# Background weight conversions in four pieces a unit, handed out inside the gated products

## The chip, the core and the metric

The kernel runs on one NeuronCore of a Trainium2 chip. The time is device microseconds of one execution. The engines that matter here are TensorE (matmuls, PE in the rows; PEld is its weight load), VectorE (DVE), ScalarE (ACT), GpSimd (POOL) and SyncE (SP), whose queue issues nearly all DMAs. Each engine takes its queue in the order in which the program emits it.

## The reference

Softcapped attention, then two MLPs on its output, in fp32 (inputs come as 64-bit floats):

```python
scores = cap * np.tanh(scale * q @ k.T / cap)              # 4 x 12 heads, 448 x 64
x = softmax(scores) @ v                                    # -> 1792 tokens x 768
g = sigmoid(x @ w_gate) * (x @ w_val)                      # "first MLP", d_ff 1536
y = g @ w_out                                              # 1792 x 768
h = y @ w_in2                                              # "second MLP", d_ff 2048
out = (h * np.cos(h)) @ w_out2                             # 1792 x 768
```

## The kernel before

The tokens go in two halves of 896 (two batches each). The order of all instructions is written out by hand: the program's order is each engine's order. First comes attention for the first half, then the gated MLP for it, `mlp1(0, ...)`, with the second half's attention beside it; then `mlp1(1, ...)`, the second gated MLP, which is the stretch that the change touches; then the cosine MLP for the second half and for the first, `mlp2(1, ...)` and `mlp2(0, ...)`.

Every product is done in three matmul passes of split fp32 operands: high weight by high input, high weight by low input, low weight by high input (`mm3`, six matmuls of 448 columns per 128 rows of contraction). So a weight tile needs a split before TensorE can use it: `w_split` lets ScalarE write the high part (L233) and GpSimd the low part (L234). A tile of gate or value weights, or half of an output column block's, feeds one product of 36 matmuls.

The weights arrive as 64-bit floats. Converting one unit of them (128 x 768 values, some units half as large) takes a raw load of 768 KB (`raw_tile`, L147), two ScalarE instructions (`signs`: Abs, L156, then Sign, L158) and four VectorE instructions (`convert`, L163 to L173). In `mlp1(0, ...)` the gated MLP's units are converted as they are used, and stored (`kept`). `mlp1(1, ...)` only loads them again (`f<-kept`, L140) and splits them. Meanwhile it converts the 34 units of the cosine MLP in the background and stores them in `kept` (L203), for both passes of `mlp2`: the first 6 units of input weights, 6 of output weights, 5, 6, 5 and 6; units 19, 22, 30 and 33 among them, counted from 0, are half-size.

`background()` is a generator; each `next(beside, None)` hands out one piece of it. A unit is three pieces: (1) Abs, Sign, the store of the unit before and the raw load of the unit after; (2) two VectorE instructions; (3) the other two. The very first piece loads the first raw tile.

`mlp1` loops over the 12 hidden units m (128 columns of d_ff each): the gate's product, its sigmoid on ScalarE, `w_step()`; the value product, gate times value on VectorE, the split of the result (`copy` on ScalarE, subtraction on VectorE), `w_step()`. `w_step` emits the split of the weights that TensorE needs two products later (`lead[0] = 2`), then, with `w_loads`, the load of the kept tile that is split two steps after. After each hidden unit come five pieces. Then come the six output blocks m, two products each, with a piece after some of the twelve contraction steps, a `w_step` after each product and the split of y at the end (copy on ScalarE, subtraction on VectorE). What is left of the background is emitted after the last block.

Kept tiles `f` and background results `fb` share four buffers (`fpool`), which go round in the order in which they were released; raw tiles and split weights share seven (`wts`).

Of the kernel before, what the change touches and what calls it, by code (L numbers as in the profile page):

```python
# [27 lines left out]
def softcap_attention_gated_mlp_cos_mlp(  # L28
# [40 lines left out]
    BESIDE = ((2, 10), (3, 2), (3, 6), (4, 1), (4, 5), (4, 8), (5, 1), (5, 5), (5, 8))  # L69


    PIECES, BESIDE_Y = 5, (0, 2, 4, 6, 8, 9, 11)

    AGAIN = (1, 2, 4, 5, 7, 8, 10, 11)

# [19 lines left out]
    def big_tile(shape, dtype, name):  # L95
        return big.tile(shape, dtype, tag="big", name=name)
# [33 lines left out]
    def f_tile(i):  # L130
        return fpool.tile([P, UW], F32, tag="f", name=f"f{i}")
# [12 lines left out]
    def raw_tile(u):  # L144
        name, src, nk, n = u
        t = wts.tile([P, UW, 2], I32, tag="w", name=f"{name}_raw")[:, : nk * n]
        nc.sync.dma_start(out=t.rearrange("p (k f) t -> p k f t", k=nk), in_=src)  # L147
        return t
# [5 lines left out]
    def signs(raw, g):  # L154
        hi = raw[..., 1].bitcast(F32)
        nc.scalar.activation(out=g, in_=hi, func=AF.Abs)  # L156
        yield
        nc.scalar.activation(out=hi, in_=hi, func=AF.Sign, bias=tiny)  # L158

    def convert(raw, g):  # L160
        lo, hi = raw[..., 0], raw[..., 1]
        gi = g.bitcast(I32)
        nc.vector.tensor_scalar(out=g, in0=g, scalar1=F64_MIN_HI, scalar2=F64_MAX_HI, op0=ALU.max, op1=ALU.min)  # L163
        yield
        nc.vector.tensor_scalar(
            out=gi, in0=gi, scalar1=4, scalar2=REBIAS, op0=ALU.logical_shift_left, op1=ALU.bitwise_xor
        )
        yield
        nc.vector.scalar_tensor_tensor(
            out=gi, in0=lo, scalar=28, in1=gi, op0=ALU.logical_shift_right, op1=ALU.bitwise_or  # L170
        )
        yield
        nc.vector.scalar_tensor_tensor(  # L173
            out=gi, in0=gi, scalar=1, in1=hi, op0=ALU.logical_shift_right, op1=ALU.bitwise_xor
        )
# [20 lines left out]
    def background():  # L196

        raw = {N1: raw_tile(unit[N1])}
        done = None

        def store():
            u, g = done
            nc.sync.dma_start(out=kept[u][:, : g.shape[1]], in_=g)  # L203
            there.add(u)

        yield
        for u in range(N1, NU):
            _, _, nk, n = unit[u]
            g = f_tile(f"b{u}")[:, : nk * n]
            for _ in signs(raw[u], g):  # L210
                pass
            if done:
                store()
            if u + 1 < NU:
                raw[u + 1] = raw_tile(unit[u + 1])
            yield
            c = convert(raw.pop(u), g)
            next(c)
            next(c)
            yield  # L220
            for _ in c:
                pass
            done = (u, g)
            yield
        store()
# [52 lines left out]
    def w_step(mid=nothing):  # L278

        w_front(mid)  # L280
        w_back()
# [22 lines left out]
    def w_catch():  # L304

        if pos["split"] < min(pos["use"] + min(3, lead[0]), pos["conv"]):
            w_back()
        if pos["conv"] < min(pos["use"] + 5, pos["split"] + 3):
            w_front()

    def w_take():
        i = pos["use"]
        pos["use"] += 1
        return w_t.pop(i)
# [190 lines left out]
    def mm3(ps, w, kk, x, first, last):  # L505

        for wi, xi in ((0, 0), (0, 1), (1, 0)):
            for c in range(BH):
                nc.tensor.matmul(  # L509
                    ps[:, c, :S],  # L510
                    lhsT=w[:, wi, kk, :],
                    rhs=x[:, xi, c, :],
                    start=(first and (wi, xi) == (0, 0)),
                    stop=(last and (wi, xi) == (1, 0)),
                )

    def ps_tile(name):
        return psS.tile([P, BH, 512], F32, tag="S", name=name)

    def tmp_tile(name):  # L520
        return tmp.tile([P, BH, S], F32, tag="tmp", name=name)

    def mlp1(hf, before, beside):

        x = [x_t[i] for i in range(KD)]
        g = []
        for m in range(KF):
            ps = {}  # L530
            for part in ("g", "v"):
                w = w_take()
                ps[part] = ps_tile(f"p{part}{hf}_{m}")
                if m == 0:
                    for kk in range(KD - 2):
                        mm3(ps[part], w, kk, x[kk], kk == 0, False)
                    if part == "g":
                        w_first = w
                        for _ in before:
                            pass  # L540
                        continue
                    for kk in (KD - 2, KD - 1):
                        mm3(ps["g"], w_first, kk, x[kk], False, kk == KD - 1)
                    sg = tmp_tile(f"sg{hf}_{m}")
                    nc.scalar.activation(out=sg, in_=ps["g"][:, :, :S], func=AF.Sigmoid)
                    w_step()
                    for kk in (KD - 2, KD - 1):
                        mm3(ps["v"], w, kk, x[kk], False, kk == KD - 1)
                else:
                    for kk in range(KD):  # L550
                        mm3(ps[part], w, kk, x[kk], kk == 0, kk == KD - 1)
                    if part == "g":
                        sg = tmp_tile(f"sg{hf}_{m}")
                        nc.scalar.activation(out=sg, in_=ps["g"][:, :, :S], func=AF.Sigmoid)
                        w_step()
            nc.vector.tensor_tensor(out=sg, in0=ps["v"][:, :, :S], in1=sg, op=ALU.mult)  # L556
            gt = big_tile([P, 2, BH, S], F32R, f"g{hf}_{m}")
            nc.scalar.copy(out=gt[:, 0], in_=sg)  # L558
            nc.vector.tensor_tensor(out=gt[:, 1], in0=sg, in1=gt[:, 0].bitcast(F32), op=ALU.subtract)
            g.append(gt)  # L560
            w_step()
            w_catch()
            if hf:
                for _ in range(PIECES):
                    next(beside, None)
        y = []
        for m in range(KD):
            ps = ps_tile(f"py{hf}_{m}")
            for s in range(2):
                w = w_take()  # L570
                for kk in range(KF // 2):
                    i = s * KF // 2 + kk
                    mm3(ps, w, kk, g[i], i == 0, i == KF - 1)
                    if hf == 0 and (m, i) in BESIDE or hf and i in BESIDE_Y:
                        next(beside, None)
                w_step()
            if hf == 0:
                yt = tmp_tile(f"y{hf}_{m}")
                nc.scalar.copy(out=yt, in_=ps[:, :, :S])
                nc.sync.dma_start(out=ykept[m], in_=yt)  # L580
                continue
            yt = big_tile([P, 2, BH, S], F32R, f"y{hf}_{m}")
            nc.scalar.copy(out=yt[:, 0], in_=ps[:, :, :S])
            nc.vector.tensor_tensor(out=yt[:, 1], in0=ps[:, :, :S], in1=yt[:, 0].bitcast(F32), op=ALU.subtract)
            y.append(yt)
        return y
# [132 lines left out]
    with tc.manual_schedule():  # L719
        nc.vector.memset(zeros, 0.0)  # L720
        nc.vector.reciprocal(out=tanh_scale, in_=cap_sb)
        nc.vector.tensor_scalar_mul(out=tanh_scale, in0=tanh_scale, scalar1=1.0 / float(D) ** 0.5)
        nc.scalar.activation(out=guard, in_=cap_sb, func=AF.Exp, scale=-1.0)
        nc.vector.tensor_scalar_mul(out=guard, in0=guard, scalar1=1e-9 / CP)
        att = [attention(hf) for hf in range(B // BH)]
        steps = 3 + (BH * NP + 1) * NC - LAST
        for _ in range(steps):
            next(att[0])
        mlp1(0, att[0], att[1])
        for _ in range(steps - len(BESIDE)):  # L730
            next(att[1])
        others = background()
        lead[0] = 2
        y = mlp1(1, att[1], others)
        y_first = []
        for _ in others:
            pass
        lead[0] = 3
        mlp2(1, y, y_again(y_first))
        mlp2(0, y_first, iter(()))  # L740
# [35 lines left out]
```

## Time and profile before

| | |
|---|---|
| time, median of 3 runs | 1235.0 us (1234.67, 1235.0, 1239.3) |
| the profiled execution: time, span | 1240.16 us, 1238.4 us |
| TensorE busy, of the span | 1208.6 us, 98% |
| VectorE, ScalarE, GpSimd busy | 55%, 48%, 36% |
| mean granted TensorE clock, of full speed | 0.993 |

Busy shares are of one profiled execution. A matmul's end is modelled, so a busy TensorE is not one at its peak; the starts of its groups of matmuls tell its pace.

### The profile page before, as it was taken

The page shows a single profiled execution, that of the slowest core. Times are in us where ns is not written, and L with a number is a line of the kernel's source. Part 1 is how long each engine was busy: PE and PEld are TensorE (multiplying, and loading weights), DVE is VectorE, ACT ScalarE, POOL GpSimd, SP SyncE. Part 2 cuts the span into 40 slices and gives each one's busy share as a digit, 9 for nine tenths or more (in the row PEclk, how much of TensorE's full clock was granted, in tenths as well). Part 3 has the DMA queues.
Part 4 walks back from the last instruction along what each step waited for, and adds up shares of the span by engine and source line. Part 5 has one row for each costly group of instructions (what it writes and reads, how often), then busy time and mean ns, then how long its engine had stood idle before and what let it go on. Part 6 is the DMA issues. An engine that isn't in the chain of part 4 may idle for free. (4 is left out here: it accounts for less than half of the span.)

```text
span 1238.4 us, 15883 instructions
## 1 busy us (share of the span) xinstructions
PE 1208.6 (98%) x6342; PEld 1037.4 (84%) x6342; DVE 682.1 (55%) x729; ACT 593.7 (48%) x664; POOL 443.4 (36%) x234
## 2 busy tenths in 40 slices
PE   8989999999999999999899899999999999999998
PEld 4445889999987546989888799999999999999998
DVE  6998698777633996555555674420423434024242
ACT  6886555445426885444343544533505335244150
POOL 2767132232314675222212221622424334235040
PEclk9999999999999999999999899999999999999999
DMA  6432465545833340455554675221121531212013
GB/s 154 126 94 69 156 209 171 167 159 164 216 129 107 90 124 1 153 167 177 179 179 155 208 248 167 64 64 43 48 77 33 167 120 52 77 32 88 22 33 96
DMA packets 127082, 148.17 MB, mean 120 GB/s; under 512 B 50080, under 2 KB 100640, under 8 KB 127008
## 3 DMA queue, kind: packets, MB, share of 16 engines
q1 hardware_dynamic: 126720, 147.09, 38.8%
q8 instruction: 50, 0.82, 0.3%
q14 instruction: 24, 0.20, 0.1%
q10 hardware_dynamic: 288, 0.07, 0.0%
HBM read 112.13 MB, written 35.00 MB: 119 GB/s over the span
## 5 line engine op out<-in xcount | busy, mean ns | idle before, releaser
L234 POOL TENSOR_TENSOR w<-f,w 128x768 fp32r<-128x768 f32 (+1 forms) x140 | 267.5, 1916 | 683.3 <-ACT w L233 598.5
L631 PE MATMUL po<-w,z 128*128 128x384 f32 x1248 | 220.8, 334 | 2.2 <-POOL w L234 2.2
L631 PEld LDWEIGHTS po<-w,z 128*128 128x128 f32 x1248 | 216.8, 188 | 3.0 <-POOL w L234 2.8
L509 PE MATMUL pg<-x,w 128*128 128x448 f32 x864 | 185.1, 372 | 7.2 <-ACT w L233 4.6
L509 PEld LDWEIGHTS pg<-x,w 128*128 128x128 f32 x864 | 164.0, 191 | 25.5 <-ACT w L233 5.7
L509 PE MATMUL py<-g,w 128*128 128x448 f32 x864 | 181.7, 371 | 3.3 <-ACT w L233 2.3
L509 PE MATMUL pv<-x,w 128*128 128x448 f32 x864 | 181.2, 367 | 1.0 <-DVE sg L556 1.0
L509 PEld LDWEIGHTS py<-g,w 128*128 128x128 f32 x864 | 163.8, 191 | 18.9 <-ACT w L233 2.6
L509 PEld LDWEIGHTS pv<-x,w 128*128 128x128 f32 x864 | 161.9, 188 | 17.3 <-issue 3.1
L233 ACT CAST w<-f 128x768 fp32r<-128x768 f32 (+1 forms) x140 | 112.1, 808 | 40.7 <-DVE f L173 16.2
L678 DVE TENSOR_SCALAR n<-u 128x896 f32<-128x896 f32 (+1 forms) x38 | 25.1, 660 | 192.7 <-ACT u L677 192.7
L509 PE MATMUL ph<-ya,w 128*128 128x448 f32 x576 | 119.5, 368 | 0.0
L509 PE MATMUL ph<-y,w 128*128 128x448 f32 x576 | 118.6, 367 | 0.0
L509 PEld LDWEIGHTS ph<-ya,w 128*128 128x128 f32 x576 | 108.1, 188 | 10.8
L509 PEld LDWEIGHTS ph<-y,w 128*128 128x128 f32 x576 | 108.1, 188 | 9.9
L391 ACT ACTIVATE p<-s,tanh_scale 112x896 f32<-112x896 f32 x96 | 93.0, 1009 | 43.5 <-PE s L388 43.4
L397 ACT ACTIVATE p<-p,cap_sb 112x1792 f32<-112x1792 f32 x48 | 86.3, 1797 | 0.1
L388 PEld LDWEIGHTS s<-st 64*112 64x112 f32 x576 | 46.4, 174 | 41.2 <-ACT p L391 19.1
L417 PE MATMUL pv<-p,v 112*64 112x448 f32 x384 | 77.5, 545 | 2.0 <-PE t L367 2.0
L558 ACT CAST g<-sg 128x896 fp32r<-128x896 f32 x24 | 22.6, 942 | 115.3 <-DVE sg L556 115.3
L388 PE MATMUL s<-st 64*112 64x448 f32 x576 | 74.4, 385 | 1.5 <-ACT p L391 1.4
L436 DVE RECIPROCAL r<-den 128x448 f32<-128x448 f32 x24 | 70.8, 2949 | 8.7 <-PE den L433 8.7
(82 smaller groups left out, 1236.0 us busy)
## 6 DMA issues: line engine op xcount, KB each, us to landing
f<-kept SPq DMA_DIRECT2D x96, 384.0 KB, 3.3
kept<-f SPq DMA_DIRECT2D x36, 384.0 KB, 2.7
wi_raw<-in_moe_w_in_dram SPq DMA_DIRECT2D x16, 768.0 KB, 6.0
kept<-fb SPq DMA_DIRECT2D x30, 384.0 KB, 2.7
wz_raw<-in_moe_w_out_dram SPq DMA_DIRECT2D x14, 768.0 KB, 5.4
wg_raw<-in_moe_w_gate_dram SPq DMA_DIRECT2D x12, 768.0 KB, 5.1
wv_raw<-in_moe_w_val_dram SPq DMA_DIRECT2D x12, 768.0 KB, 5.0
wo_raw<-in_moe_w_out_dram SPq DMA_DIRECT2D x12, 768.0 KB, 4.8
```

The costliest lines, as they stand in the source:

```text
L233: nc.scalar.copy(out=t[:, 0], in_=r)
L234: nc.gpsimd.tensor_tensor(out=t[:, 1], in0=r, in1=t[:, 0].bitcast(F32), op=ALU.subtract)
L388: nc.tensor.matmul(ps[:CP, h, :S], lhsT=st[r, ki, ks], rhs=st[r, qi], start=(n == 0), stop=(n == 2))
L391: nc.scalar.activation(out=pt[:CP, j], in_=ps[:CP, :, :S], func=AF.Tanh, scale=tanh_scale[:CP])
L397: nc.scalar.activation(out=pt[:CP], in_=pt[:CP], func=AF.Exp, scale=cap_sb[:CP])
L417: nc.tensor.matmul(pv[h * D : (h + 1) * D, :S], lhsT=tv[:, h, c, :], rhs=pt[:CP, j, h, :], start=(c == 0), stop=(c == NC - 1),)
L436: nc.vector.reciprocal(out=r[:, 0], in_=den[:, :S])
L509: nc.tensor.matmul(ps[:, c, :S], lhsT=w[:, wi, kk, :], rhs=x[:, xi, c, :], start=(first and (wi, xi) == (0, 0)), stop=(last and (wi, xi) = ...
L558: nc.scalar.copy(out=gt[:, 0], in_=sg)
L631: nc.tensor.matmul(pos_t[t][:, :NB], lhsT=zf[kk][:, zi, t * P : (t + 1) * P], rhs=ws[kk // UK][:, wi, kk % UK, :], start=(kk == 0 and (zi, ...
L678: nc.vector.tensor_scalar_add(out=n[:, c], in0=u[:, c], scalar1=ROUND)
```

## The change

Background units are handed out in four pieces instead of three: (1) Abs and the store of the unit before; (2) Sign and the raw load of the unit after; (3) and (4) two VectorE instructions each. In the gated part, instead of five pieces after each hidden unit, there are seven inside the products of each hidden unit from the second on: after contraction steps 1, 3 and 5 of the gate's product and after 0, 2, 4 and 5 of the value product. In the output part there are nine pieces per block instead of seven. Together they are 131 pieces where there were 102, of 137 (before: 103) and a last store; the rest is emitted at the end.

```diff
-    PIECES, BESIDE_Y = 5, (0, 2, 4, 6, 8, 9, 11)
+    BESIDE_G, BESIDE_Y = ((1, 3, 5), (0, 2, 4, 5)), (0, 2, 3, 4, 6, 7, 8, 10, 11)
...
             g = f_tile(f"b{u}")[:, : nk * n]
-            for _ in signs(raw[u], g):
-                pass
+            c = signs(raw[u], g)
+            next(c)
             if done:
                 store()
+            yield
+            for _ in c:
+                pass
             if u + 1 < NU:
                 raw[u + 1] = raw_tile(unit[u + 1])
             yield
...
                     for kk in range(KD):
                         mm3(ps[part], w, kk, x[kk], kk == 0, kk == KD - 1)
+                        if hf and kk in BESIDE_G[part == "v"]:
+                            next(beside, None)
...
             w_step()
             w_catch()
-            if hf:
-                for _ in range(PIECES):
-                    next(beside, None)
```

## Rows read from the trace of the kernel before

**Rows 1.** The page, its head: the span, and TensorE's busy time.

```profile
span 1238.4 us, 15883 instructions
...
PE 1208.6 (98%) x6342; PEld 1037.4 (84%) x6342; DVE 682.1 (55%) x729; ACT 593.7 (48%) x664; POOL 443.4 (36%) x234
```

**Rows 2.** TensorE's timeline: start, us, instructions [idle before <- releaser], second gated MLP.

```profile
494.73 7.46 PE L509 MATMUL pg<-x,w 128*128 128x448 f32 x36
...
545.80 7.46 PE L509 MATMUL pv<-x,w 128*128 128x448 f32 x36
...
562.64 7.46 PE L509 MATMUL pv<-x,w 128*128 128x448 f32 x36
...
591.83 7.46 PE L509 MATMUL pv<-x,w 128*128 128x448 f32 x36
601.56 1.07 PE L509 MATMUL pg<-x,w 128*128 128x448 f32 x4 [2.28 <-ACT w L233]
...
611.65 7.46 PE L509 MATMUL pv<-x,w 128*128 128x448 f32 x36
...
640.83 7.46 PE L509 MATMUL pv<-x,w 128*128 128x448 f32 x36
...
659.66 7.46 PE L509 MATMUL pv<-x,w 128*128 128x448 f32 x36
666.96 14.76 PE L509 MATMUL py<-g,w 128*128 128x448 f32 x72
683.97 1.09 PE L509 MATMUL py<-g,w 128*128 128x448 f32 x4 [2.26 <-ACT w L233]
...
761.14 19.21 PE L509 MATMUL ph<-y,w 128*128 128x448 f32 x94
```

**Rows 3.** Windows: stretch, its length, busy time by engine, granted clock, DMA share, GB/s.

```profile
605.00:610.00 5.00, 5.00 (x22) 4.56 (x21) 4.86 (x6) 1.97 (x2) 1.11 (x1) 0.81 0.17 67
...
685.00:690.00 5.00, 3.98 (x12) 3.48 (x12) 4.63 (x5) 3.49 (x4) 2.12 (x2) 0.54 0.47 150
```

**Rows 4.** Timelines of ScalarE and GpSimd, second gated MLP.

```profile
550.57 0.90 ACT L156 ACTIVATE fb<-wz_raw 128x768 f32<-128x768 f32 x1 [4.87 <-DMA wz_raw<-in_moe_w_out_dram]
...
553.20 0.83 ACT L233 CAST w<-f 128x768 fp32r<-128x768 f32 x1
...
681.28 0.89 ACT L156 ACTIVATE fb<-wz_raw 128x768 f32<-128x768 f32 x1 [7.88 <-DMA wz_raw<-in_moe_w_out_dram]
...
510.74 0.94 ACT L558 CAST g<-sg 128x896 fp32r<-128x896 f32 x1 [6.88 <-DVE sg L556]
511.59 0.83 ACT L233 CAST w<-f 128x768 fp32r<-128x768 f32 x1
...
512.50 2.01 POOL L234 TENSOR_TENSOR w<-f,w 128x768 fp32r<-128x768 f32 x1 [6.71 <-ACT w L233]
```

**Rows 5.** SyncE's queue, timeline: a store, and the loads behind it.

```profile
517.53 0.32 SPq L203 DMA_DIRECT2D kept<-fb  x1
...
520.29 0.80 SPq L140 DMA_DIRECT2D f<-kept  x2
```

**Rows 6.** Page, DMA issues (median us to landing); then landings of wz_raw, of wi_raw.

```profile
wi_raw<-in_moe_w_in_dram SPq DMA_DIRECT2D x16, 768.0 KB, 6.0
kept<-fb SPq DMA_DIRECT2D x30, 384.0 KB, 2.7
wz_raw<-in_moe_w_out_dram SPq DMA_DIRECT2D x14, 768.0 KB, 5.4
...
DMA to landing us min/median/max: 3.4/4.9/7.6
...
DMA to landing us min/median/max: 5.0/6.0/9.6
```

**Rows 7.** VectorE's timeline: the first and the last of one unit's four conversions.

```profile
512.73 2.20 DVE L163 TENSOR_SCALAR fb<-fb 128x768 f32<-128x768 f32 x1
...
516.55 0.96 DVE L173 SCALAR_TENSOR_TENSOR fb<-fb,wi_raw 128x768 int32<-128x768 int32 x1
```

**Rows 8.** Timelines of VectorE and TensorE in the cosine MLP's first group.

```profile
770.49 0.63 DVE L678 TENSOR_SCALAR n<-u 128x896 f32<-128x896 f32 x1 [6.05 <-ACT u L677]
...
807.65 7.40 PE L631 MATMUL po<-w,z 128*128 128x384 f32 x41 [1.33 <-POOL w L234]
```

## The prediction

> **What bounds the kernel now.** I read the page first, then TensorE's timeline of the second gated MLP, then what ScalarE, GpSimd and SyncE did around each hole in it. The profiled execution spans 1238.4 us [rows 1] and its time is 1240.16 us, 1.76 us around the span; the three runs have a median of 1235.0, so the profile is one of the longer executions, 5.2 us above it. TensorE is the bound (the page has it busy 98%), so only holes in its stream are worth anything.
>
> In the stretch that the change touches, a product of 36 matmuls takes 7.30 us when nothing is late: seven products from 494.73 to 545.80 [rows 2]. By that rhythm the stretch from 494.73 to the cosine MLP's start at 761.14, 22 gated products and 432 output matmuls, is worth (22 + 12) x 7.30 = 248.1 us; it took 266.4. **18.3 us are lost, in four places** [rows 2]:
> - A: from 545.80 to 562.64 is 16.84 us for two products of 14.59: 2.25.
> - B: 591.83 to 611.65 is 19.82: 5.23.
> - C: 640.83 to 659.66 is 18.83: 4.24.
> - D: 666.96 to 761.14 is 94.18 for twelve products of 87.56: 6.6.
>
> At B and D the row behind the hole says the wait was for ScalarE's split of the weights (2.28 and 2.26 us); GpSimd's low part follows. The rest of B and D is clock: the granted clock was 0.81 in 605 to 610 and 0.54 in 685 to 690, after TensorE had stood still [rows 3], so part of it ran at 1.2 instead of 2.4 GHz.
>
> Why is the split late? ScalarE takes its queue in order. At A the first instruction of a background unit (Abs) waited 4.87 us for the raw weights' load until 550.57, and behind it stood Sign, the sigmoid and at 553.20 the split, which TensorE wanted at 553.10. At D the Abs waited 7.88 us until 681.28 [rows 4]. The reader is to see why: five pieces in one lump after a hidden unit hold two units' Abs, sometimes where the last lump had two as well, with no TensorE-gated instruction between them, while a raw load takes 5.4 to 6.0 us [rows 6]. A, B and C lie three hidden units apart, which is 15 pieces or five background units: the same alignment each time.
>
> **The change part by part.** *Instructions.* None is added or removed: 34 units keep two ScalarE, four VectorE instructions, a load and a store each. The two ScalarE instructions go into separate pieces, and the load of the next unit moves from the first piece to the second, behind Sign.
>
> *Gated products.* Seven pieces go out per hidden unit, three ahead of the sigmoid, four ahead of the gate's product, from the second unit on. Four pieces are one unit, so a gated product never holds two Abs, and each Abs is parted from the next by an instruction gated on TensorE. An Abs that waits for its load now waits while ScalarE would be waiting for the sigmoid's product anyway (6.88 us of idle time before the 510.74 row [rows 4]). That removes A, B and C: 11.7 us.
>
> Where could they come back? I walked the queue orders. A split after the value product goes: copy of g 1.42 us after the product's end (510.74 against 509.32), split, then GpSimd until 514.51 [rows 4]: 5.2 us of 7.30, and 0.81 more because the first four matmuls use the high part alone. In hidden units 2, 6 and 10 (from 0) the value product holds Sign of one unit, its conversions, then Abs of the next, so the raw load is issued in that product and wanted in it. It also stands on SyncE's queue behind a load of kept weights that takes the slot of the unit just stored, and so waits until that store has landed (517.53 to 520.29 shows such a wait, 2.76 us [rows 5]). That store waits for the conversion, which ends 8.2 us into the gate product (512.73 to 517.51 in the same place [rows 7]). So: 8.2 + 0.3 + 2.7 + 0.5 = 11.7, which is 4.4 us into the value product; the load lands 5.4 to 6.0 later, at 9.8 to 10.4; Abs 0.9, copy to split 0.85, split to GpSimd 0.9 and GpSimd 2.0 [rows 4] add 4.7: 14.5 to 15.1. TensorE wants it at 14.6 + 0.8 = 15.4. It just fits; I take nothing, with bounds of nothing and three holes like A (6.7), since the longest loads were 7.6 and 9.6 us [rows 6].
>
> *Output products.* Nine pieces in each twelve steps instead of seven of three-piece units: 2.25 units per 14.59 us where there were 2.33. D goes, because unit 19 begins on loads that landed early: 6.6 us. But this stage has no TensorE-gated instruction except the copy of y, so ScalarE runs at the pace of the loads. The chain over two units is Abs 0.9, conversion 4.8 [rows 4, 7], store issue 0.3, raw issue 0.4, landing 5.4 to 6.0 [rows 6]: 12.1 on average, against 8 pieces x 14.59 / 9 = 12.97 allotted. It fits, with 0.9 to spare. In four places (units 21, 22, 30, 31) the first and the second piece fall in different products; there the raw load stands behind a load of kept weights, which waits for the store's landing: 3.1 us more, 15.2, an overrun of 2.2. The first two meet half-size units (19 and 22), which win it back. The last two come at the end: the split and the copy of the last y stand behind unit 32's Abs, whose load, stepped along SyncE's queue with these durations, lands 90.4 to 91.9 us after the stage's start; Abs, Sign, split and copy are 3.6 more, so y's high part would be ready at 94 to 95.5 where TensorE wants it at 93.7, its low part one us later. I give back 2.5 us for the stage, with bounds of nothing (all loads at 5 us) and two holes of D's size (13).
>
> The Trainium skill speaks against this order: DMA: Bandwidth & Descriptors, section "Anatomy of one DMA", says that completion and not setup makes up most of a transfer's fixed cost, and that HBM as target is the slowest. The store's 2.7 us for 384 KB [rows 6] agrees with its fit (2.0 us and the bytes at 436 GB/s, an estimate of 2.9). For a raw load the same fit, made for another issuing path, gives an estimate of 3.8 us where the rows have 5.4 to 6.0; by it nothing would be late in this stage, the sum would be 1224.3, and the first rival below would be the likelier way. I go by the rows.
>
> *After the stage.* Before, two VectorE instructions of the last unit were left over at the end. Now unit 32's four and the whole of unit 33 (half size) are: a set and a half where half-size halves stood, and two ScalarE instructions behind a wait for the raw load. They stand in front of the cosine MLP's first instructions, whose VectorE part had 6.05 us of idle time before 770.49 [rows 8]. That idle time is the cover, but the last y comes late too: its low part is done at about 96, a set and a half of conversions (4.8 at most for a full one, some 3.3 with GpSimd idle, my estimate) ends at 101, and VectorE is wanted 2.05 us after the first product's end (770.49 against 761.14 + 7.30), which the late y puts at 96.5: 98.6. So the chain of the first hidden unit starts 2.4 us late; bounds are nothing and the whole set and a half, 7. TensorE doesn't feel it there; it does at the group's end, where it already waits 1.33 us for a split (807.65 [rows 8]), since ScalarE, VectorE and GpSimd take turns there with no more to spare than that. I add 2.4.
>
> **Sum**, on the profiled execution: 1240.16 - 11.7 - 6.6 + 0 + 2.5 + 2.4 = 1226.8. Against the median of 1235.0 that is 8 us, 0.66%. The long executions most likely differ from the short ones in the clock after these holes, which is in the 18.3; if so, they all come down to the same time. If not, the median would come to some 5 us less.
>
> **The rivals.**
> *Nothing is given back.* The loads keep up in the output products, and the leftovers hide in the first product: 1240.16 - 18.3 = 1221.9. For it: the present output stage, with 2.33 units per 14.59 us, had no hole after D. Against it: the four places where the load now waits behind a store's landing.
> *The holes move.* Raw loads of 7 us and over make the three value products late (A to C come back, 2.25 to 5.2 each, 11.7 at most), and one D comes back with the copy of y: 1234 to 1240, no change. For it: the longest loads of 7.6 and 9.6. Against it: in these products at most one raw load is under way, and medians are 5.4 and 6.0.
> *Slower: the output stage starves.* SyncE's order of store, landing, kept load, raw load makes each Abs late, and with it each split behind it; the clock falls after each hole. Price: D's 6.6 each. It decides at three such holes (19.8 against the 18.3 won), 1241.7; four give 1248. For it: no gate between Abs and split in this stage, and four overruns of 2.2. Against it: the average chain fits with 0.9 us to spare, and a hole gives the loads time to catch up.
>
> **How the numbers follow.** A measurement of this kernel can tell about 0.5%, 6.2 us: under 1228.8 is faster, over 1241.2 slower. Forecast 0.50, between 1224 and 1232, of which 0.36 lies under 1228.8; nothing given back 0.20; holes move 0.22; starving 0.08. Faster 0.56, same 0.14 + 0.22 = 0.36, slower 0.08. The range of 8 in 10 is 1220 to 1237: it leaves out starving, the upper part of the moved holes, and a little below 1222.
>
> **What would show it.** Right: no wait of TensorE for a weight split between 494 and the last gated product, products 7.30 us apart, granted clock 1.00 there; Abs with at most one per product; raw loads issued 4 us into the value products of hidden units 2, 6 and 10. In the output stage, holes of a us or two near its end, the last y's copy some 7 us after its product, and a wait of 3 to 4 us at the first group's end in place of 1.33. Wrong: a wait for the split in value products, a granted clock under 1 in the output stage, or a copy of the last y as early as now.

## The result, and the profile after

The changed kernel takes 1224.66 us (median of 4 runs, 1222.13 to 1227.05); the kernel before, with a fourth run beside it, 1237.15 (1234.67 to 1243.52). The ratio is 0.9891, with a 95% interval from 0.9844 to 0.9938: faster by 1.1%. The profiled execution took 1222.13 us, 18.0 less than the one shown of before. The forecast was 1226.8 by its sum, in a range of 1220 to 1237. Among the executions of the kernel before beside the experiments below, one was slow (1311.74 us at a granted clock of 0.851) and is left out of the ratios.

The head of the page, for the kernel after (against [rows 1]):

```profile
span 1220.3 us, 15888 instructions
...
PE 1198.6 (98%) x6342; PEld 1033.8 (85%) x6342; DVE 685.8 (56%) x729; ACT 592.3 (49%) x664; POOL 443.3 (36%) x234
```

TensorE's timeline of the kernel after, the same stretch as [rows 2] and the first row of the cosine MLP's group as in [rows 8]. Three lines were added in the file, so L509 is now L512, and the split's lines are L236 and L237:

```profile
490.46 7.46 PE L512 MATMUL pg<-x,w 128*128 128x448 f32 x36
...
643.68 7.46 PE L512 MATMUL pv<-x,w 128*128 128x448 f32 x36
650.98 87.75 PE L512 MATMUL py<-g,w 128*128 128x448 f32 x432
738.57 6.25 PE L512 MATMUL ph<-y,w 128*128 128x448 f32 x30
746.68 0.68 PE L512 MATMUL ph<-y,w 128*128 128x448 f32 x2 [1.87 <-ACT y L585]
747.81 39.13 PE L512 MATMUL ph<-y,w 128*128 128x448 f32 x184 [0.45 <-DVE y L586]
...
789.78 7.41 PE L633 MATMUL po<-w,z 128*128 128x384 f32 x41 [1.62 <-POOL w L237]
```

The reader is to see three things. No gated product waits for a weight split any more: 22 of them take 160.52 us (490.46 to 650.98), which is 22 times 7.30. The 432 output matmuls are one unbroken row of 87.75 us. And there is one new hole, behind 738.57: the first product of the cosine MLP waits for the last y, its high part and then its low part.

Cut into stages at these starts, the two executions compare so (us, from the starts in TensorE's timelines and the ends of the two spans):

| stretch | before | after | difference |
|---|---|---|---|
| from the span's start up to the second hidden unit of the second gated MLP | 494.73 | 490.46 | -4.27 |
| its 22 products | 172.23 | 160.52 | -11.71 |
| the 12 output products | 94.18 | 87.59 | -6.59 |
| the cosine MLP's start, to its group's end [rows 8] | 46.51 | 51.21 | +4.70 |
| from there to the end | 430.75 | 430.52 | -0.23 |

The last four rows sum to -13.8. The first, 4.27, lies ahead of all that the change touches. A second execution of the same changed kernel (below) enters the stage at 494.52, so this part isn't the change's.

The new hole is costed at more than its two waits of 1.87 and 0.45 us, for the clock goes down behind it. Windows of the kernel after (stretch, length, busy time of each engine, granted clock, DMA share, GB/s):

```profile
745.00:750.00 5.00, 2.87 (x9) 2.25 (x10) 3.23 (x5) 3.49 (x6) 1.82 (x1) 0.82 0.26 82
750.00:755.00 5.00, 5.00 (x23) 4.57 (x22) 4.18 (x7) 3.04 (x4) 0.00 (x0) 0.83 0.47 147
```

Mean granted clocks of 0.82 and 0.83 are stretches spent partly at 1.2 and partly at 2.4 GHz, as at B and D before [rows 3]. So the 4.70 is 2.32 of waiting, 0.29 more at the group's end (1.62 for 1.33), and the remaining 2.1 falls in the stretch of the lowered clock (0.18 and 0.17 of two windows of 5 us are 1.75 of it).

Why is y late? The timelines of ScalarE, GpSimd and SyncE of the kernel after, around it, and who SyncE's loads of kept weights (L140) waited for longest between 725 and 745:

```profile
733.31 0.89 ACT L156 ACTIVATE fb<-wz_raw 128x768 f32<-128x768 f32 x1 [5.14 <-DMA wz_raw<-in_moe_w_out_dram]
734.10 0.82 ACT L236 CAST w<-f 128x768 fp32r<-128x768 f32 x1
...
743.22 0.89 ACT L156 ACTIVATE fb<-wz_raw 128x768 f32<-128x768 f32 x1 [7.39 <-DMA wz_raw<-in_moe_w_out_dram]
744.14 0.97 ACT L158 ACTIVATE wz_raw<-wz_raw,tiny 128x768 f32<-128x768 f32 x1
745.02 0.81 ACT L236 CAST w<-f 128x768 fp32r<-128x768 f32 x1
745.74 0.89 ACT L585 CAST y<-py 128x896 fp32r<-128x896 f32 x1
```

```profile
735.06 2.05 POOL L237 TENSOR_TENSOR w<-f,w 128x768 fp32r<-128x768 f32 x1 [6.25 <-ACT w L236]
```

```profile
730.70 0.32 SPq L203 DMA_DIRECT2D kept<-fb  x1
737.13 0.32 SPq L140 DMA_DIRECT2D f<-kept  x1
737.50 0.44 SPq L147 DMA_DIRECT2D wz_raw<-in_moe_w_out_dram  x1
```

```profile
SPq L140 <- POOL w L237: 6.0, 1, 6.0
```

The raw load is issued at 737.50, behind a load of kept weights that goes out 6.4 us after the last store. It lands as the Abs begins, at 743.22, 5.7 us after its issue; split and copy of y stand behind that Abs. The product that makes the last y was over at 738.57.

The load of kept weights did not wait for that store, which landed 3.0 us after its issue. It waited 6.0 us for GpSimd, which reads the buffer that the load is to fill until its split ends at 737.11. That split was late because ScalarE's part of it, at 734.10, stood behind the Abs of 733.31, and that Abs had waited 5.14 us for a raw load of its own. So the delay goes round: raw load, Abs, split on ScalarE, split on GpSimd, load of kept weights, next raw load.

### The profile page after: what moved, and what is told of

It reads as the page before. It is cut to its first block, busy times and chain, and to the rows that moved or that the text cites. A ratio compares the mean times of both kernels' runs of the same rounds, so it can differ in the third digit from the quotient of the medians.

```text
span 1220.3 us, 15888 instructions
## 1 busy us (share of the span) xinstructions
PE 1198.6 (98%) x6342; PEld 1033.8 (85%) x6342; DVE 685.8 (56%) x729; ACT 592.3 (49%) x664; POOL 443.3 (36%) x234
## 4 chain that ended last, share of the span: by engine, by line
PE 74%; DVE 13%; DMA 5%; ACT 4%; issue 3%; SPq 1%; POOL 0%; DVEq 0%; ACTq 0%; POOLq 0%
PE po L633 17%; PE ph L512 16%; PE pv L512 12%; PE pg L512 11%; PE py L512 7%; PE pv L420 4%; PE s L391 3%; DMA wz_raw<-in_moe_w_out_dram 2%; DVE r L439 2%; PE more L633 1%; DMA wi_raw<-in_moe_w_in_dram 1%; PE t L370 1%; DVE f L169 1%; DVE fb L169 1%; PE den L436 1%
## 5 line engine op out<-in xcount | busy, mean ns | idle before, releaser
L237 POOL TENSOR_TENSOR w<-f,w 128x768 fp32r<-128x768 f32 (+1 forms) x140 | 267.3, 1915 | 666.1 <-ACT w L236 570.2
L512 PE MATMUL pv<-x,w 128*128 128x448 f32 x864 | 180.0, 366 | 1.0 <-DVE sg L561 1.0
L512 PE MATMUL pg<-x,w 128*128 128x448 f32 x864 | 179.8, 366 | 0.0
L512 PE MATMUL py<-g,w 128*128 128x448 f32 x864 | 177.5, 366 | 0.0
L512 PEld LDWEIGHTS pv<-x,w 128*128 128x128 f32 x864 | 162.0, 188 | 16.0 <-issue 3.1
L512 PEld LDWEIGHTS pg<-x,w 128*128 128x128 f32 x864 | 162.0, 188 | 14.6 <-issue 0.7
L512 PEld LDWEIGHTS py<-g,w 128*128 128x128 f32 x864 | 161.6, 188 | 13.7 <-issue 1.0
L236 ACT CAST w<-f 128x768 fp32r<-128x768 f32 (+1 forms) x140 | 112.1, 808 | 40.5 <-DVE f L173 16.2
L512 PE MATMUL ph<-y,w 128*128 128x448 f32 x576 | 120.8, 371 | 2.3 <-ACT y L585 1.9
L512 PEld LDWEIGHTS ph<-y,w 128*128 128x128 f32 x576 | 109.2, 190 | 13.3 <-ACT y L585 2.2
L512 PE MATMUL ph<-ya,w 128*128 128x448 f32 x576 | 119.5, 368 | 0.0
L512 PEld LDWEIGHTS ph<-ya,w 128*128 128x128 f32 x576 | 108.1, 188 | 10.8
L404 POOL TENSOR_TENSOR sum<-p 112x896 f32<-112x896 f32 x24 | 55.8, 2327 | 48.7 <-ACT p L400 23.8
```

The source lines that it names most:

```text
L236: nc.scalar.copy(out=t[:, 0], in_=r)
L237: nc.gpsimd.tensor_tensor(out=t[:, 1], in0=r, in1=t[:, 0].bitcast(F32), op=ALU.subtract)
L404: nc.gpsimd.tensor_tensor(out=s, in0=pt[:CP, 1] if half == 0 else s, in1=pt[:CP, 0], op=ALU.add)
L512: nc.tensor.matmul(ps[:, c, :S], lhsT=w[:, wi, kk, :], rhs=x[:, xi, c, :], start=(first and (wi, xi) == (0, 0)), stop=(last and (wi, xi) = ...
```

## The experiments

Each experiment is an edit of the changed kernel. The first four share the runs of the kernel before on one occasion (median 1239.13, 7 runs), the last four those on another (median 1238.92, 11 runs).

**The changed kernel again.** No edit.

> The changed kernel once more, beside the others. 1222 to 1227 us, no hole in the gated products; one hole where the cosine MLP's first product waits for the last y (1.9 and 0.4 us in the first profile, about 4.4 us late with the clock behind it).

Measured: 1229.12 us (1226.66 to 1232.93, 4 runs), ratio 0.9922 (0.9898 to 0.9946); the profiled execution 1232.93, nearly 11 above the first profile of the same kernel. Both parts of the expectation failed, the time by 2 us and the holes by their place. TensorE's timeline of this run:

```profile
538.30 7.46 PE L512 MATMUL pg<-x,w 128*128 128x448 f32 x36
545.59 0.98 PE L512 MATMUL pv<-x,w 128*128 128x448 f32 x4
547.51 6.88 PE L512 MATMUL pv<-x,w 128*128 128x448 f32 x32 [0.94 <-POOL w L237]
554.23 7.60 PE L512 MATMUL pg<-x,w 128*128 128x448 f32 x36
561.67 7.60 PE L512 MATMUL pv<-x,w 128*128 128x448 f32 x36
...
667.38 28.64 PE L512 MATMUL py<-g,w 128*128 128x448 f32 x140 [0.56 <-POOL w L237]
697.87 1.08 PE L512 MATMUL py<-g,w 128*128 128x448 f32 x4 [1.85 <-ACT w L236]
```

Its stages: 163.87 gated, 95.44 output, 46.66 cosine start. A hole is back in a value product, and the output part has two. Two more things are to be seen here. First, the products are 7.30 us apart up to the hole and 7.44 behind it (554.23 to 561.67), with the granted clock at 1.00 in 500 to 540 and in 555 to 600; more on that at the end. Second, where the hole comes from. ScalarE and SyncE of the same run:

```profile
538.52 0.89 ACT L156 ACTIVATE fb<-wi_raw 128x768 f32<-128x768 f32 x1 [5.68 <-DMA kept<-fb]
...
543.69 0.94 ACT L563 CAST g<-sg 128x896 fp32r<-128x896 f32 x1 [3.23 <-DVE sg L561]
544.54 0.83 ACT L236 CAST w<-f 128x768 fp32r<-128x768 f32 x1
```

```profile
535.67 0.32 SPq L203 DMA_DIRECT2D kept<-fb  x1
```

The Abs of 538.52 doesn't wait for its raw load but for the landing of a store (`kept<-fb`, issued at 535.67): its result takes the buffer that this store empties. Conversion and gate product of VectorE, the copy of g and the split follow late, one behind the other. The first profile of the changed kernel has the same wait at the same place, 3.94 us long where this one is 5.68, and just escapes.

The difference is made ahead of that store, in the conversion whose result it writes. VectorE and GpSimd in the first profile, then in this one:

```profile
528.92 0.96 DVE L173 SCALAR_TENSOR_TENSOR fb<-fb,wi_raw 128x768 int32<-128x768 int32 x1
...
528.92 2.67 POOL L237 TENSOR_TENSOR w<-f,w 128x768 fp32r<-128x768 f32 x1 [2.11 <-ACT w L236]
```

```profile
533.04 2.60 DVE L173 SCALAR_TENSOR_TENSOR fb<-fb,wi_raw 128x768 int32<-128x768 int32 x1
...
532.97 1.85 POOL L237 TENSOR_TENSOR w<-f,w 128x768 fp32r<-128x768 f32 x1 [2.05 <-ACT w L236]
```

In both, the last instruction of the conversion and a split on GpSimd begin within 0.1 us of each other. In the first profile GpSimd's takes 2.67 us and VectorE's 0.96; here GpSimd begins 0.07 us ahead and takes 1.85, and VectorE's takes 2.60. Up to there the two executions run 4.12 us apart (528.92 and 533.04), from the store on 5.76 (529.91 and 535.67), and the split had 0.65 us to spare. So this one meeting of two engines decides the hole; that the one engine holds up the other is inferred from these rows.

**Three pieces a unit, spread out.** Three pieces as before, so the raw load goes out in the first, right behind the store; five pieces per hidden unit, inside the products; the output part as before.

```diff
-    BESIDE_G, BESIDE_Y = ((1, 3, 5), (0, 2, 4, 5)), (0, 2, 3, 4, 6, 7, 8, 10, 11)
+    BESIDE_G, BESIDE_Y = ((1, 4), (0, 2, 4)), (0, 2, 4, 6, 8, 9, 11)
...
-            c = signs(raw[u], g)
-            next(c)
+            for _ in signs(raw[u], g):
+                pass
             if done:
                 store()
-            yield
-            for _ in c:
-                pass
...
             w_catch()
+            if hf and m == 0:
+                for _ in range(5):
+                    next(beside, None)
```

> Only the placing: units stay in three pieces, with the raw load behind the store as before, the five pieces of a hidden unit go inside its products (two and three), the first hidden unit keeps its lump, and the output stage is that of before (7 pieces a block). Theory (a split is late only because two Abs stand on ScalarE between two instructions that TensorE gates): A to D are gone, the stretch from the second hidden unit to the last output product is 248 us, and since no raw load stands behind a store's landing the last y comes on time: 1218 to 1221, 4 to 5 us under the changed kernel. Rival (the fourth piece, Sign and load apart from Abs, is what helps): holes for a split remain in the gated products, 1230 to 1237.

Measured: 1220.68 us (1217.85 to 1223.27, 4 runs), ratio 0.9857 (0.9829 to 0.9884), 8.4 below the changed kernel beside it. TensorE:

```profile
651.88 87.71 PE L509 MATMUL py<-g,w 128*128 128x448 f32 x432
739.43 43.94 PE L509 MATMUL ph<-y,w 128*128 128x448 f32 x216
...
786.00 7.38 PE L633 MATMUL po<-w,z 128*128 128x384 f32 x41 [1.39 <-POOL w L234]
```

Stages 160.52, 87.55 and 46.57: every hole of before is gone, and the one at 738.57 doesn't arise; the whole first product of the cosine MLP is one row. So four pieces aren't needed for the gain, and the order of the load in them costs.

**Four pieces a unit, in a lump.** The pieces of the changed kernel, seven of them after each hidden unit from the second on, none inside the products.

```diff
-                        if hf and kk in BESIDE_G[part == "v"]:
-                            next(beside, None)
...
             w_catch()
+            if hf and m:
+                for _ in range(7):
+                    next(beside, None)
```

> Only the fourth piece: seven pieces of four to a unit, in one lump after each hidden unit from the second on. Theory: three lumps of four hold two Abs, so more holes than before, three to eight of 2.2 to 5.2 us in the gated products, and the late last y on top: 1232 to 1255. Rival (the fourth piece is what helps): no such holes, 1224.

Measured: 1238.01 us (one run, inside the range that the theory gave), where the kernel before has 1239.13. TensorE's holes in the gated products:

```profile
537.28 1.08 PE L512 MATMUL pg<-x,w 128*128 128x448 f32 x4 [1.24 <-ACT w L236]
...
585.23 1.08 PE L512 MATMUL pg<-x,w 128*128 128x448 f32 x4 [0.55 <-ACT w L236]
...
602.70 6.75 PE L512 MATMUL pg<-x,w 128*128 128x448 f32 x32 [0.65 <-POOL w L237]
...
647.20 1.09 PE L512 MATMUL pg<-x,w 128*128 128x448 f32 x4 [1.27 <-ACT w L236]
```

Stages 171.81, 94.72 and 47.92: the holes come back, at other hidden units than A to C. Twelve of the 22 products ran at 7.44 us instead of 7.30, so some 9.6 us of the 171.81 are holes, where the kernel before had 11.7. The gain in the gated products lies in where the pieces are handed out, not in how many a unit is cut into.

**The raw load in the first piece.** The changed kernel with one move: the load of the next raw tile goes back to right behind the store.

```diff
             if done:
                 store()
+            if u + 1 < NU:
+                raw[u + 1] = raw_tile(unit[u + 1])
             yield
             for _ in c:
                 pass
-            if u + 1 < NU:
-                raw[u + 1] = raw_tile(unit[u + 1])
```

> The changed kernel with the raw load back in the first piece, right behind the store, ahead of the load of kept weights in SyncE's queue. Theory (the last y is late because the raw load waits behind a kept load that waits for a store's landing): the last y's copy comes within 3 us of its product's end, the hole at the cosine MLP's start is gone, 1218 to 1221, 4 to 5 us under the changed kernel. Rival (the output stage is late because ScalarE and VectorE have too much to do at nine pieces a block, or because the leftovers are): the hole stays, 1222 to 1227.

Measured: 1220.65 us (1217.96 to 1226.98, 4 runs), ratio 0.9858 (0.9823 to 0.9893): the time of three pieces spread. SyncE, with the raw load whose Abs stands ahead of the last y's copy, ScalarE and TensorE:

```profile
734.91 0.32 SPq L203 DMA_DIRECT2D kept<-fb  x1
735.33 0.39 SPq L147 DMA_DIRECT2D wz_raw<-in_moe_w_out_dram  x1
735.80 0.46 SPq L140 DMA_DIRECT2D f<-kept  x1
```

```profile
744.35 0.91 ACT L585 CAST y<-py 128x896 fp32r<-128x896 f32 x1 [1.72 <-PE py L512]
```

```profile
744.15 44.80 PE L512 MATMUL ph<-y,w 128*128 128x448 f32 x216
...
790.82 7.40 PE L633 MATMUL po<-w,z 128*128 128x384 f32 x41 [0.64 <-POOL w L237]
```

That raw load (735.33) goes out right behind the store and ahead of the load of kept weights, the copy of the last y waits for nothing but its product, and the hole is gone: the stage to the group's end takes 46.67 against 51.21, although at the slower pace. So the raw load's place behind the load of kept weights is the cause of the hole. What that load waits for, this experiment can't tell; the theory's "store's landing" is not what the changed kernel's trace shows there (GpSimd, 6.0 us).

**The raw load in the third piece.** The other way: one piece later than in the change, ahead of the conversion.

```diff
             for _ in c:
                 pass
+            yield
             if u + 1 < NU:
                 raw[u + 1] = raw_tile(unit[u + 1])
-            yield
             c = convert(raw.pop(u), g)
```

> The changed kernel with the raw load one piece later, in the third piece, ahead of the conversions: the suspected wait of the output stage made longer, and more raw loads behind a kept load on SyncE's queue. Theory (the changed kernel's remaining holes come from raw loads that stand behind a store's landing): the value products lose their margin of 0.65 us and over, holes for a split come into some of them and into the output stage, three or more, 1232 to 1245. Rival (what is left depends on the amount of work and not on the load's place): one hole as in the changed kernel, 1222 to 1229.

Measured: 1230.96 us (one run), a little below what was expected. TensorE:

```profile
708.47 1.08 PE L512 MATMUL py<-g,w 128*128 128x448 f32 x4 [1.23 <-ACT w L236]
...
755.23 0.68 PE L512 MATMUL ph<-y,w 128*128 128x448 f32 x2 [2.84 <-ACT y L585]
```

The later load costs at the places that the theory names, in the output part (91.14, with a hole for a split) and at the last y (2.84 us and a stage of 52.2). At both, the load of kept weights ahead of the raw load waited for GpSimd (3.3 us until 699.22, 6.0 until 745.42) and not for a store. The other half of the expectation failed: the gated products have no hole (163.68, all at 7.44), so there the load's place isn't what decides.

**More left over.** The load in the first piece, and eight instead of nine pieces per output block, so that twelve pieces are emitted at the end instead of six.

```diff
-    BESIDE_G, BESIDE_Y = ((1, 3, 5), (0, 2, 4, 5)), (0, 2, 3, 4, 6, 7, 8, 10, 11)
+    BESIDE_G, BESIDE_Y = ((1, 3, 5), (0, 2, 4, 5)), (0, 2, 3, 4, 6, 7, 9, 10)
```

> The kernel with the raw load in the first piece, but eight pieces instead of nine in each output block, so that twelve pieces (two units and a half) instead of six are left for the end. Theory (leftovers are free as long as they fit into the cosine MLP's first product, where ScalarE and VectorE have 5 to 6 us to spare, and cost what is over): two more units with their raw loads, some 8 us of waits on ScalarE, don't fit; the wait at the first group's end grows from 0.6 us to 4 to 8, and the time is 1222 to 1230. Rival (leftovers never reach TensorE): 1217 to 1223 as without them.

Measured: 1220.51 us (one run), below the theory's range and inside the rival's. TensorE:

```profile
754.52 1.08 PE L512 MATMUL ph<-y,w 128*128 128x448 f32 x4 [0.97 <-ACT w L236]
756.62 28.64 PE L512 MATMUL ph<-y,w 128*128 128x448 f32 x140 [1.01 <-POOL w L237]
...
788.16 7.40 PE L633 MATMUL po<-w,z 128*128 128x384 f32 x41 [1.63 <-POOL w L237]
```

Twice the leftovers cost 49.36 for that stage against 46.57 for three spread at the same pace, 2.8 us, part of it in waits for a split at the third cosine product; less than was expected, and not only at the group's end. So the trace speaks for a cost, which the time of one run can't show. Six leftovers with y on time cost nothing that shows: with the load in the first piece the group's end waits 0.64 and the stage takes 46.67, and the changed kernel's second profile, whose y wasn't late, has 46.66. Three spread, with one piece left over, has 46.67 at the same pace (its second profile, below).

**Three spread and the changed kernel, once more.** The same two kernels again, side by side.

> Three pieces a unit spread inside the products, as before, measured in more rounds against the changed kernel beside it. Theory: no hole for a split at any time, 1217 to 1224, 5 to 9 us under the changed kernel. Rival (the two differ only by chance): within 2 us of it.

> The changed kernel in more rounds. 1222 to 1233, since its margins of 0.65 us let a hole come and go between executions.

Measured: three spread 1223.07 us (1221.43 to 1226.58, 5 runs), ratio 0.9882 (0.9855 to 0.991); the changed kernel 1227.05 (1225.8 to 1227.6, 6 runs), ratio 0.991 (0.9885 to 0.9936). Three pieces are ahead again, by 4.0, a little less than the 5 to 9 expected. The order is the same as before, its size isn't. This profiled execution of three spread took 1223.06 where the first took 1218.41, with no hole in either:

```profile
490.77 7.60 PE L509 MATMUL pg<-x,w 128*128 128x448 f32 x36
...
654.45 89.44 PE L509 MATMUL py<-g,w 128*128 128x448 f32 x432
743.73 44.80 PE L509 MATMUL ph<-y,w 128*128 128x448 f32 x216
```

Its gated and output products take 163.68 + 89.28 against 160.52 + 87.55: 4.9 us for the same instructions at the same granted clock.

## Why the prediction came out right, step by step

**A, B, C: right.** Forecast 11.7, measured 11.71 in the first profile, which has the pace of the one before; the other two have the slower pace in most or all of these products. The lump was the cause: four pieces in a lump keep the holes, three pieces spread remove them, and two more profiles of the changed kernel have one hole and none in the 22 products. ScalarE's Abs now waits 7.16 us for its load (522.25 in the first profile of after) while nothing that TensorE needs is late.

**The three value products of hidden units 2, 6 and 10: right to cost nothing.** I had the load landing 9.8 to 10.4 us into the product. The Abs began 9.9 us into hidden unit 2's (522.25, product from 512.35), and 8.9 into the other two. **But the danger stood elsewhere.** At hidden units 3, 7 and 11 the Abs waits for a buffer, not for its load: its target is the one that a store is just emptying, 3.94, 2.77 and 2.78 us in the first profile, with 0.65 us to spare for the split behind the first of them. My walk through the queues followed the four shared buffers for the loads of kept weights, but not for the results of Abs. In the second profile that margin was gone, by the meeting of VectorE and GpSimd shown above, and a hole stood there. Of the three runs with a profile of the changed kernel one has this hole, so the rival that the holes move is true of some executions.

**D: right in two of three profiles.** Forecast 6.6, measured 6.59, and the third profile of the changed kernel has no hole there either. The second has two, and a stage of 95.44, no less than before, some 1.7 of it the slower pace. The first of them comes of the same meeting once more, at hidden unit 11 (a conversion's last instruction, from 653.00, took 2.57 us beside GpSimd's split from 652.92). The second is the round of the last y: a load of kept weights waited 4.4 us for GpSimd (until 688.99), and the raw load behind it landed just ahead of the Abs of 695.21, with split and copy of y behind that. Why the round closed there in this one of the three executions stays open. The last y was on time in it, the stage being longer by its holes.

**The output part's give-back: right in place, wrong in the wait, low in size.** The place is the one named: unit 32's Abs in front of the split and the copy of the last y, its load behind a load of kept weights. I had the load landing 90.4 to 91.9 us after the stage's start and y's high part at 94 to 95.5; it landed at 92.2 (743.22 against 650.98) and the copy ended at 95.7. But my walk had the load of kept weights waiting for a store's landing, and it waited for GpSimd, in this profile (6.0 us) and in the third (5.4). The store had landed at 733.7 (730.70 and 3.0). Had the load waited for that alone, the raw load would have gone out at 734.1 and landed at 739.7, and the copy of y would have ended at 743.1, where TensorE ran out at 744.8: no hole, by an estimate from these rows. The store's landing does come in one unit earlier: the load ahead of unit 31's raw load waited 2.0 us for one. That my landing came so near is therefore partly luck.

The Trainium skill's fit (DMA: Bandwidth & Descriptors, section "Anatomy of one DMA"), made for another issuing path, gave an estimate of 3.8 us for such a load. This one took 5.7, so the measurement speaks for the rows. Of the term, 2.5 against some 4.4, I had left out the clock behind the hole: 2.32 of waiting became 4.4. The load in the first piece removes it; the load in the third makes the stage 5.5 longer than that (52.2 against 46.67, both at 7.44) and adds 1.9 in the output part (91.14 against 89.27).

**The leftovers: wrong in size.** Forecast 2.4 at the group's end, measured 0.29. The two profiles with six leftovers and y on time (46.66 and 46.67) show no cost at all against 46.67 with one, at the same pace. Twelve cost 2.8, about what I had charged for six. The two terms were off in opposite ways, and their sum, 4.9 against 4.70, was right by luck. With it, the three stages gained 13.6 us in the first profile where 13.4 were forecast; in the second and third profile of the changed kernel they gained 6.95 and 10.31, for holes and the slower pace.

**The long executions: wrong.** I took the 5 us between the profiled execution and the median for clock behind the holes. Three pieces spread, with no hole in these products, differs between two profiled executions by about as much (1218.41 and 1223.06), through the pace of the matmuls. Before's profile has the slower pace in the first gated MLP and the faster one in the second, so part of its length had nothing to do with the holes, and the sum made on it took that along: ahead of the stage the first profile of after is 4.27 shorter, which is most of the 4.7 (1226.8 - 1222.13) by which the sum missed that execution. That the unprofiled executions spread for the same reason is likely, but only argued.

**Better than both.** Three pieces spread (1220.68 and 1223.07) take 8.4 and 4.0 us less than the changed kernel beside them, and the change with the load in the first piece (1220.65) 8.5. With the pace equal (7.30 us products), three spread and the first profile of after differ by 4.68 in these stages (294.64 against 299.32), and all but 0.04 of it is the cosine MLP's start.

## What to carry to other kernels

Hand background work out between the instructions that gate the busy engine, not in a lump behind them: the spacing decided here, and the size of the pieces didn't. Before moving a load in a queue, look at what it then stands behind: a load that waits for its buffer, be it for a store's landing or for an engine that still reads it, holds up each load queued after it. Ask the trace what a late load waited for before giving the cause: here the nearest store was not it. When you walk a queue by hand, include the buffers that stores, loads and engines share, and put the lowered clock behind a hole into the hole's price.

## What was not expected of the hardware

With the granted clock at 1.00, TensorE runs these products at one of two paces: 36 matmuls in 7.30 us or in 7.44 (203 or 207 ns each). Windows of three spread, its first and its second profile, with the number of matmuls in each 50 us beside their busy time:

```profile
500.00:550.00 50.00, 50.00 (x249) 46.33 (x248) 28.40 (x32) 21.79 (x25) 14.97 (x7) 1.00 0.68 221
```

```profile
500.00:550.00 50.00, 50.00 (x244) 45.41 (x243) 27.63 (x31) 21.43 (x25) 14.57 (x7) 1.00 0.67 219
```

249 against 244, the same clock, the same instructions. In these profiles the pace held over long stretches. Some changes came across a pause of TensorE: at the hole of 545.59 in the changed kernel's second profile it went from 7.30 to 7.44, and in the lump's run the other way, at the hole after 585.23. Others came where no pause is shown: in four profiles (the lump, the load first, the load third, the third of the changed kernel) the first 24 matmuls of the first gate product took 5.12 or 5.13 us and those of its value product, some 9 us later, 5.22. In the third profile of the changed kernel it also changed within the output products (88.31 us for a stage that takes 87.6 or 89.3). What sets it stays open. It is worth 5 us in this stage alone, more than some of the terms that were argued over here, so executions should be compared stage by stage at the same pace.
